# One expert's second, third and fourth tile as a single tile of 320 columns

## The chip, the cores and the metric

The kernel runs on one core of a Trainium2 chip. The core has a matrix engine (TensorE, PE in the profile; its weight loads are listed as PEld), VectorE (DVE), ScalarE (ACT), GpSimd (POOL) and SyncE (SP), which run their own queues of instructions and wait for each other by semaphores. The metric is the device time of one execution in microseconds, the median of several runs.

## The reference

Attention with 32 global and 512 local tokens per batch comes first, then a feed-forward layer with a squared ReLU, then eight routed experts, which are all that the change touches:

```python
def _moe2_ref(x, w_skip, w_gate, w1, w2):          # x: 2176 x 512
    do_compute = x @ w_skip > 0
    out = x.copy()
    xc = x[do_compute]
    logits = xc @ w_gate                            # 8 experts
    e_idx = np.argmax(logits, axis=1)
    probs = softmax(logits)
    gate_w = probs[np.arange(len(xc)), e_idx]
    for e in range(8):
        mask = e_idx == e
        h = np.maximum(xc[mask] @ w1[e], 0.0)       # 512 -> 1024
        y[mask] = gate_w[mask, None] * (h @ w2[e])  # 1024 -> 512
    out[do_compute] = xc + y
```

With the reference's inputs the experts 0 to 7 get 337, 24, 22, 433, 82, 126, 86 and 133 tokens. Expert 3, with 433, is the one that has more than three tiles of 128.

## The kernel before

Each float32 operand of the experts is split into a high part, rounded to the format fp32r that TensorE multiplies fast, and a low part, the rest; a product takes three matmuls (high by high, high by low, low by high). The weights come in eight pieces of 512 KB per expert (`fetch_expert`, on the SP queue), are cast to their high part on ScalarE and subtracted to their low part on VectorE (`convert_expert`; tiles e24h, e24l and so on, eight numbers per expert). `work` spreads this over the steps u of the first tile of an expert, for five pieces of the next expert ahead.

A tile of 128 tokens goes through `gather` (an indirect DMA on GpSimd by the token list), `prepare` (four transposes on TensorE, a copy for the high part on ScalarE, a subtraction for the low part on VectorE) and `expert_tile`: tokens are the stationary operand, weights move with 512 columns (48 matmuls in all), and between the layers the hidden row block is transposed (eight transposes) and split again. The result is multiplied by the gate, added to x (line 950) and scattered to the output (line 954).

How many tiles an expert takes is known only when the kernel runs, so all tiles behind the first stand in nested branches: `more(e, 1)` runs tile 1 if the count is over 128; `more_two(e)` runs tile 2 alone, or, over 384 tokens, tiles 2 and 3 as a pair of 256 columns (`expert_pair`: the weights are stationary in the first layer, the tokens in the second); then tile 4 and a loop. The rows of tile 1 are prepared at step 5 of tile 0, and those of tiles 2 and 3 are gathered and prepared inside tile 1. TensorE's queue is told ahead which way a branch goes by a hint placed by hand (`hint`, at step 0 of the tile before and four steps from the end of the pair).

Everything is emitted in one order written out by hand (`tc.manual_schedule`), so an engine does its work in the order of the lines in the code. The stage around the change is `run(range(AFTER, E), ...)` in the arm `few`, which treats experts 1 and 2 (at most 32 tokens each) in a short form, and then runs the experts 3 to 7 in turn. Tiles of the arm have names ending in `_a`. [...]

Of the kernel before, what the change touches and what calls it, by code (L numbers as in the profile page):

```python
# [54 lines left out]
def attention_ffn_routed_experts(  # L55
# [755 lines left out]
    PARTS_AT = {0: (0, 1), 1: (2,), 2: (3,), 3: (4,), 4: (5,), 5: (6,), 6: (7,)}  # L811
    U0, U1 = 6, 5
    FEW, AFTER = (1, 2), 3
    raws, spare, shared = {}, [], {}

    def give(n):
# [58 lines left out]

    def prepared(e, j):
        if j > 1:
            return [x[:, :, j % 2 * P:(j % 2 + 1) * P] for x in joint()]
        x = xps[(0, e % 2) if j == 0 else (1, 0)]
        return x[:, 0], x[:, 1]  # L880

    def gather(e, j, gi):
        nc.gpsimd.indirect_dma_start(  # L883
# [4 lines left out]
    def prepare(e, j):  # L888
        tr = pair(f"etr_{e}_{j}")
        transposes(tr, gathered(e, j))  # L890
        split(*prepared(e, j), tr)

    def inner(in_arm, z, name):
        tag = ("s", "o")[z % 2] if in_arm else "h"
# [2 lines left out]
    def expert_tile(e, j, si):  # L897

        name = f"{e}_{j}"
        xg, (ph, pl) = gathered(e, j), prepared(e, j)  # L900
        hs, rs = [None] * 2, [None] * 2
        hl = sb("kT", 1, [P, NPAIR, S], f"ehl_{name}").rearrange("p a s -> p (a s)")[:, 0:2 * KE * P].bitcast(F32R)
        gh, gl = (hl[:, z * KE * P:(z + 1) * KE * P].rearrange("p (f k) -> p f k", f=KE) for z in range(2))
        y = ps.tile([P, DM], F32, tag="x2", bufs=2, name=f"y_{name}{arm[0]}")

        def first(fb, k0, k1):
            if k0 == 0:
                hs[fb] = inner(j > (not e), fb, f"eh_{name}_{fb}")
            h = hs[fb]
            for k in range(k0, k1):  # L910
                wh, wl = ew[e, 1, (fb, k)]
                nc.tensor.matmul(h, lhsT=ph[:, k, :], rhs=wh, start=(k == 0), stop=False)
                nc.tensor.matmul(h, lhsT=ph[:, k, :], rhs=wl, start=False, stop=False)
                nc.tensor.matmul(h, lhsT=pl[:, k, :], rhs=wh, start=False, stop=(k == KD - 1))
            if k1 == KD:
                rs[fb] = sb("sm", 2, [P, S], f"er_{name}_{fb}")[:, 0:512]
                nc.scalar.activation(rs[fb], h, AF.Relu)

        def turn(fb):
            tr = pair(f"ertr_{name}_{fb}")  # L920
            transposes(tr, rs[fb])
            split(gh[:, 4 * fb:4 * fb + 4, :], gl[:, 4 * fb:4 * fb + 4, :], tr)

        def second(f0, f1):
            for f in range(f0, f1):
                wh, wl = ew[e, 2, f]
# [145 lines left out]
    with tc.manual_schedule():  # L1072
# [187 lines left out]
        def more(e, j):  # L1260

            if j == UNROLL:
                with tc.For_i(UNROLL, (n_tok[e] + (P - 1)) // P, 1) as it:
                    gi = sb("gi", 2, [P, 1], f"gi{e}", I32)
                    nc.vector.tensor_copy(gi, gidx[:, bass.ds(it + e * TPE, 1)])
                    si = sb("si", 2, [P, 1], f"si{e}", I32)
                    nc.vector.tensor_copy(si, sidx[:, bass.ds(it + e * TPE, 1)])
                    gather(e, UNROLL, gi)
                    prepare(e, UNROLL)
                    for _ in expert_tile(e, UNROLL, si):  # L1270
                        pass
                return
            with tc.If(n_tok[e] > least(e, j), label=f"more{e}_{j}{arm[0]}") as branch:
                if e and j == 4:
                    gather(e, j, slot(gidx, e, j))
                    prepare(e, j)
                    following = ()
                else:
                    following = (2, 3) if e else range(j + 1, UNROLL)[:1]
                for z in following:  # L1280
                    if (e, z) != (0, 3):
# [28 lines left out]
        def run(experts, later=(), ahead=NST - 1, late=U0):  # L1310
            later = list(later)
            for e in experts:
                for u, _ in enumerate(expert_tile(e, 0, slot(sidx, e, 0))):
                    if u in HINTS:
                        hint(e, 1, HINTS[u])
                    if u == U1:
                        prepare(e, 1)
                        if e == E - 1:
                            prepare_rest(e, 1)
                    if u == (U0 if e != experts[0] else late) and e + 1 < E:  # L1320
                        prepare(e + 1, 0)
                    work(e, u, ahead if e == experts[0] else NST - 1)
                    if later:
                        later.pop(0)()
                more(e, 1)

        more(0, 2)
        carried = dict(est), dict(raws)
        shared.update((n, raws[n]) for n in est)
        with tc.If(n_tok[E] <= SEG, label="few") as few:  # L1330
            arm[0] = "_a"
            both_o = sb("xt", 1, [P, 3 * BLK], "eo_few")[0:2 * SEG, 0:DM]
            both_si = sb("hi_i", 2, [P, 1], "si_few", I32)[0:2 * SEG]
            rests = []
# [71 lines left out]
```

## Time and profile before

| | us |
|---|---|
| median of 3 runs | 719.64 (717.83 to 722.03) |
| the profiled execution | 719.74 |
| its span, first to last instruction | 718.0 |
| TensorE busy in the span | 689.4 |
| VectorE busy in the span | 398.7 |
| ScalarE busy in the span | 369.8 |

The profile is of one execution. A time in it counts from the start of the span. A row of the timeline gives the start, the duration, the engine, the line of the code, the operation, the tiles written and read and, in brackets, how long the engine stood idle before and who released it. Matmuls overlap, so their pace is read from their starts. An engine's name with a q stands for its queue: branches, register and semaphore operations.

### The profile page before, as it was taken

How to read it: one execution, taken by the hardware profiler on the slowest of the kernel's cores; microseconds unless marked ns; L12 is line 12 of the kernel's file. 1: busy time of each engine (PE TensorE's matmuls, PEld its weight loads, DVE VectorE, ACT ScalarE, POOL GpSimd, SP SyncE). 2: the span in 40 equal slices, each digit the busy share in tenths (PEclk: the TensorE clock that was granted, in tenths of full speed). 3: DMA queues.
4: the chain of work that ended last, by engine and by line, in shares of the span. 5: the costliest groups of instructions: out<-in, count | busy, mean ns of one | idle time of the engine just before them, and what ended most of it. 6: DMA issues, size and time to landing. Idle time of an engine off the chain costs nothing.

```text
span 718.0 us, 18725 instructions
## 1 busy us (share of the span) xinstructions
PE 689.4 (96%) x7613; PEld 575.8 (80%) x7613; DVE 398.7 (56%) x1067; ACT 369.8 (52%) x943; POOL 165.1 (23%) x209
## 2 busy tenths in 40 slices
PE   7689998999999999999999999999999999999995
PEld 4566677888888988888898898888977887897773
DVE  1889955762654255365336436525267527517993
ACT  5767567665534654444355453534336226416880
POOL 5000053463112221221122212122215224202211
PEclk9799999999999999999999999999999999999999
DMA  9999552064064303115530403110048599905910
GB/s 273 256 294 313 190 132 61 2 167 85 2 145 113 83 32 73 44 36 111 132 65 32 108 2 112 49 59 31 31 147 267 164 324 360 388 26 185 358 34 24
DMA packets 119161, 95.31 MB, mean 133 GB/s; under 512 B 84885, under 2 KB 92053, under 8 KB 119044
## 3 DMA queue, kind: packets, MB, share of 16 engines
q1 hardware_dynamic: 108352, 71.01, 35.3%
q10 hardware_dynamic: 8292, 15.48, 6.5%
q0 software_dynamic: 2400, 7.28, 3.0%
q8 instruction: 71, 1.16, 0.7%
q14 instruction: 46, 0.38, 0.2%
HBM read 81.49 MB, written 12.79 MB: 131 GB/s over the span
## 4 chain that ended last, share of the span: by engine, by line
PE 70%; DMA 17%; issue 5%; DVE 3%; SPq 1%; ACT 1%; POOL 1%; POOLq 0%; ACTq 0%; DVEq 0%
DMA xg<-x2d,slots 15%; PE h L700 8%; PE acc L725 7%; PE acc L727 7%; PE h L702 7%; PE h L701 7%; PE acc L726 7%; PE sc L413 3%; PE acc L723 3%; PE h L697 3%; PE po L451 2%; PE ptr L442 2%; PE gsa L485 1%; PE qtr L341 1%; PE x2tr L280 1%
## 5 line engine op out<-in xcount | busy, mean ns | idle before, releaser
L184 POOL TENSOR_TENSOR gl<-g,gh 128x256 fp32r<-128x256 f32 x107 | 79.5, 743 | 303.1 <-ACT gh L183 146.1
L700 PE MATMUL h<-xh,w_in 128*128 128x256 f32 x464 | 135.0, 291 | 0.7 <-ACT xh L183 0.7
L701 PE MATMUL h<-xl,w_in 128*128 128x256 f32 x464 | 129.7, 280 | 0.3 <-DVE xl L184 0.3
L702 PE MATMUL h<-xh,w_in 128*128 128x256 f32 x464 | 129.8, 280 | 0.0
L725 PE MATMUL acc<-w_out,gh 128*128 128x512 f32 x232 | 97.6, 421 | 1.5 <-ACT gh L183 1.5
L727 PE MATMUL acc<-w_out,gl 128*128 128x512 f32 x232 | 92.0, 396 | 0.2
L726 PE MATMUL acc<-w_out,gh 128*128 128x512 f32 x232 | 91.7, 395 | 0.0
L700 PEld LDWEIGHTS h<-xh,w_in 128*128 128x128 f32 x464 | 87.1, 188 | 4.3 <-ACT xh L183 0.9
L701 PEld LDWEIGHTS h<-xl,w_in 128*128 128x128 f32 x464 | 87.3, 188 | 2.6 <-DVE xl L184 0.5
L704 ACT ACTIVATE g<-h 128x256 f32<-128x256 f32 x128 | 48.7, 381 | 77.0 <-PE h L702 45.7
L702 PEld LDWEIGHTS h<-xh,w_in 128*128 128x128 f32 x464 | 87.1, 188 | 0.0
L433 ACT ACTIVATE sm<-sm,mx 128x128 f32<-128x128 f32 x120 | 46.7, 391 | 49.8 <-DVE mx L431 49.8
L741 DVE TENSOR_TENSOR g<-h,g 128x256 f32<-128x256 f32 x53 | 22.3, 420 | 85.5 <-ACT g L704 85.4
L183 ACT CAST gh<-g 128x256 fp32r<-128x256 f32 x116 | 47.2, 407 | 42.2 <-DVE g L741 40.2
L727 PEld LDWEIGHTS acc<-w_out,gl 128*128 128x128 f32 x232 | 43.5, 188 | 11.9 <-POOL gl L184 1.4
L725 PEld LDWEIGHTS acc<-w_out,gh 128*128 128x128 f32 x232 | 43.6, 188 | 8.6 <-ACT gh L183 1.9
L726 PEld LDWEIGHTS acc<-w_out,gh 128*128 128x128 f32 x232 | 43.8, 189 | 5.7
L426 DVE TENSOR_TENSOR sm<-sc,mask 128x512 f32<-128x512 f32 x30 | 20.6, 688 | 23.9 <-PE sc L413 23.2
L255 POOL TENSOR_TENSOR w_in<-st_raw_in,w_in 128x512 fp32r<-128x512 f32 x10 | 13.0, 1309 | 80.6 <-ACT w_in L251 80.6
L883 POOL DMA_INDIRECT xg<-x2d,slots x16 | 20.0, 1250 | 42.8 <-DVE slots L800 13.1
L413 PEld LDWEIGHTS sc<-kT,qT 64*32 64x32 f32 x2048 | 25.5, 110 | 4.3 <-issue 3.5
L743 ACT ACTIVATE g<-g 128x256 f32<-128x256 f32 x63 | 26.2, 417 | 4.5 <-ACT g L704 2.5
(671 smaller groups left out, 1481.0 us busy)
## 6 DMA issues: line engine op xcount, KB each, us to landing
st_e<-in_moe_w_dram SPq DMA_DIRECT2D x46, 512.0 KB, 7.1
vr<-in_v_l_dram SPq DMA_DIRECT2D x49, 192.0 KB, 4.4
st_raw_in<-in_moe_w_in_dram SPq DMA_DIRECT2D x16, 512.0 KB, 6.7
st_raw_out<-in_moe_w_out_dram SPq DMA_DIRECT2D x16, 512.0 KB, 8.3
st_e<-in_moe_w_dram ACTq DMA_DIRECT2D x12, 512.0 KB, 5.4
x2d<-x ACTq DMA_DIRECT2D x19, 256.5 KB, 3.5
st_gv<-in_v_l_dram SPq DMA_DIRECT2D x8, 512.0 KB, 4.5
out_dram<-x ACTq DMA_DIRECT2D x16, 256.0 KB, 3.5
```

The source lines that it names most:

```text
L183: nc.scalar.copy(hi, src)
L184: (lo_engine or nc.vector).tensor_tensor(out=lo, in0=src, in1=hi.bitcast(F32), op=ALU.subtract)
L413: nc.tensor.matmul(scs[g][SEG * i:SEG * (i + 1), p, cols], lhsT=q[rows, p, SEG * i:SEG * (i + 1)], rhs=kT[b][rows, p, keys], start=True, s ...
L433: nc.scalar.activation(sm[:, hh, :], sm[:, hh, :], AF.Exp, bias=mx[:, hh:hh + 1], scale=SCALE, accum_out=osum[:, 2 * hh + g:2 * hh + g + 1],)
L700: nc.tensor.matmul(h, lhsT=wh, rhs=xh[:, k, :], start=(k == 0), stop=False)
L701: nc.tensor.matmul(h, lhsT=wh, rhs=xl[:, k, :], start=False, stop=False)
L702: nc.tensor.matmul(h, lhsT=wl, rhs=xh[:, k, :], start=False, stop=(k == KD - 1))
L704: nc.scalar.activation(g, h, AF.Relu)
L725: nc.tensor.matmul(acc[z], lhsT=gh[:, c], rhs=wh, start=first_one, stop=False)
L726: nc.tensor.matmul(acc[z], lhsT=gh[:, c], rhs=wl, start=False, stop=False)
L727: nc.tensor.matmul(acc[z], lhsT=gl[:, c], rhs=wh, start=False, stop=last_one)
L743: nc.scalar.activation(square, g, AF.Square)
```

## The change

If expert 3 has 385 to 448 tokens (`wide_count`: seven half tiles), its tiles 1, 2 and 3 are worked as one tile of 320 columns, the third of them with 64 rows.

- The rows of tiles 2 and 3 are gathered at the start of the arm (`gather_wide`), and all three tiles are transposed and split at the steps 5, 6 and 7 of tile 0 (`prepare_wide`: two copies on ScalarE and three subtractions on VectorE for each).
- `wide_tile` has the weights stationary in both layers and 320 token columns moving, so the hidden block needs no transposes between the layers. The second layer's result comes out transposed, in four PSUM tiles of 128 x 320. It is copied to SBUF (two blocks by VectorE, two by ScalarE), turned by twelve transposes, multiplied by the gate and added to x in three steps on VectorE, and scattered in three indirect DMAs.
- The old path, `more(e, 1)`, stands in the `Else` of the branch. The hint at step 0 of tile 0 goes to the new branch.
- `prepared` returns lists of column blocks, and the matmuls of `expert_tile` index them so; the operands are the same.

```diff
+    WIDE = 2 * P + P // 2
...
+    def gather_wide(e):
+
+        gather(e, 2, slot(gidx, e, 2))
+        wide_x[e] = sb("x2", 2, [P, ROW], f"xg_wide{e}")[0:P // 2]
+        nc.gpsimd.indirect_dma_start(
+            out=wide_x[e], out_offset=None, in_=x2d,
+            in_offset=bass.IndirectOffsetOnAxis(ap=slot(gidx, e, 3)[0:P // 2], axis=0),
+            bounds_check=NTOK - 1, oob_is_err=False,
+        )
+
+    def prepare_wide(e, j):
+
+        n = P // 2 if j == 3 else P
+        cols = slice((j - 1) * P, (j - 1) * P + n)
+        tr = pair(f"etr_{e}_{j}w")
+        transposes(tr, wide_x[e] if j == 3 else gathered(e, j), n)
+        high, low = ([x[:, :, cols] for x in xs] for xs in wide_slices())
+        for z in range(2):
+            nc.scalar.copy(high[z], tr[:, 2 * z:2 * z + 2, 0:n])
+        for l, h, k in ((low[0], high[0][:, 0:1], 0), (low[1], high[0][:, 1:2], 1), (low[2], high[1], 2)):
+            w = l.shape[1]
+            nc.vector.tensor_tensor(out=l, in0=tr[:, k:k + w, 0:n], in1=h.bitcast(F32), op=ALU.subtract)
+
+    def wide_tile(e):
+
+        xh, xl = wide_inputs(0, WIDE)
+        gs, yt = {}, []
+
+        def first(f):
+            fb, c = divmod(f * P, DM)
+            h = inner(True, f, f"ewh_{e}_{f}")[:, 0:WIDE]
+            for k in range(KD):
+                wh, wl = (w[:, c:c + P] for w in ew[e, 1, (fb, k)])
+                nc.tensor.matmul(h, lhsT=wh, rhs=xh[k], start=(k == 0), stop=False)
+                nc.tensor.matmul(h, lhsT=wh, rhs=xl[k], start=False, stop=False)
+                nc.tensor.matmul(h, lhsT=wl, rhs=xh[k], start=False, stop=(k == KD - 1))
...
+            nc.scalar.activation(gh, h, AF.Relu)
+            nc.vector.scalar_tensor_tensor(
+                out=gl, in0=h, scalar=0.0, in1=gh.bitcast(F32), op0=ALU.max, op1=ALU.subtract
+            )
+
+        def second(f):
...
+            for d in range(KD):
+                wh, wl = (w[:, d * P:(d + 1) * P] for w in ew[e, 2, f])
+                nc.tensor.matmul(yt[d], lhsT=wh, rhs=gh, start=(f == 0), stop=False)
+                nc.tensor.matmul(yt[d], lhsT=wl, rhs=gh, start=False, stop=False)
+                nc.tensor.matmul(yt[d], lhsT=wh, rhs=gl, start=False, stop=(f == KE - 1))
+
+        first(0)
+        for f in range(KE):
+            if f + 1 < KE:
+                first(f + 1)
+            second(f)
...
+        trs = [pair(f"ewtr_{e}_{t}") for t in range(2)]
+        trs.append(inner(True, 0, f"ewtr_{e}_2").rearrange("p (d c) -> p d c", d=KD))
+        for d in range(KD):
+            if d < 2:
+                nc.vector.tensor_copy(ys[:, d], yt[d])
+            else:
+                nc.scalar.copy(ys[:, d], yt[d])
+            for t in range(3):
+                n = P // 2 if t == 2 else P
+                nc.tensor.transpose(trs[t][0:n, d, :], ys[:, d, t * P:t * P + n], ident)
...
+        for t, o in enumerate(os):
+            xg = wide_x[e] if t == 2 else gathered(e, t + 1)
+            n = xg.shape[0]
+            nc.vector.scalar_tensor_tensor(
+                out=o, in0=trs[t].rearrange("p d c -> p (d c)")[0:n], scalar=xg[:, DM:DM + 1], in1=xg[:, 0:DM],
+                op0=ALU.mult, op1=ALU.add,
+            )
+        for t, o in enumerate(os):
+            scatter_rest(o, slot(sidx, e, t + 1)[0:o.shape[0]])
...
                     if u in HINTS:
-                        hint(e, 1, HINTS[u])
-                    if u == U1:
+                        if is_wide(e):
+                            tc.mark_branch_hint_location(f"wide{e}", hint=wide_count(e), engines=HINTS[u])
+                        else:
+                            hint(e, 1, HINTS[u])
+                    if is_wide(e):
+                        if U1 <= u < U1 + 3:
+                            prepare_wide(e, u - U1 + 1)
+                    elif u == U1:
                         prepare(e, 1)
...
-                more(e, 1)
+                if is_wide(e):
+                    with tc.If(wide_count(e), label=f"wide{e}") as wide:
+                        wide_tile(e)
+                    with wide.Else():
+                        more(e, 1)
+                else:
+                    more(e, 1)
+
+        def wide_count(e):
+            return (n_tok[e] + (P // 2 - 1)) // (P // 2) == 7
...
             arm[0] = "_a"
+            gather_wide(AFTER)
```


## Rows read from the trace of the kernel before

**Rows 1.** Page, first part: busy time, share and instructions of each engine.

```profile
PE 689.4 (96%) x7613; PEld 575.8 (80%) x7613; DVE 398.7 (56%) x1067; ACT 369.8 (52%) x943; POOL 165.1 (23%) x209
```

**Rows 2.** By stretch: length, busy PE PEld DVE ACT POOL, PEclk, DMA share, GB/s.

```profile
614.81:627.74 12.93, 12.93 (x68) 10.66 (x66) 4.59 (x7) 4.13 (x7) 3.05 (x3) 1.00 1.04 389
627.74:651.02 23.28, 22.83 (x145) 20.09 (x143) 5.38 (x12) 3.39 (x9) 1.11 (x2) 1.00 0.08 29
651.02:664.34 13.32, 13.17 (x64) 10.54 (x65) 11.34 (x13) 10.77 (x14) 4.71 (x4) 1.00 0.79 254
```

**Rows 3.** Timeline of PE in the pair: matmuls of 256, then of 512 columns.

```profile
628.14 0.28 PE L972 MATMUL eph_a<-xp,e24l_a 128*128 128x256 f32 x1
...
630.73 0.40 PE L986 MATMUL yp_a<-e28h_a,egh_a 128*128 128x512 f32 x1
...
632.13 0.28 PE L970 MATMUL eph_a<-xp,e24h_a 128*128 128x256 f32 x1
```

**Rows 4.** Timeline of PE at the two edges of the stage.

```profile
614.46 0.60 PE L280 MATMUL etr_a<-ident,xg 128*128 128x128 f32 x4
614.81 0.48 PE L912 MATMUL eh_a<-e24h_a,xp 128*128 128x512 f32 x1
...
650.18 0.40 PE L988 MATMUL yp_a<-e31h_a,egl_a 128*128 128x512 f32 x1
651.02 0.50 PE L912 MATMUL eh_a<-e32h_a,xp 128*128 128x512 f32 x1 [0.45 <-PEq L1273]
```

**Rows 5.** Groups by line and shape, in 614.81 to 651.02.

```profile
L975 DVE SCALAR_TENSOR_TENSOR egl_a<-eph_a,egh_a 128x256 fp32r<-128x256 f32 x8 | 3.4, 425 | 16.6 <-ACT egh_a L974 16.6
L974 ACT ACTIVATE egh_a<-eph_a 128x256 fp32r<-128x256 f32 x8 | 3.1, 384 | 18.0 <-PE eph_a L972 18.0
...
L184 DVE TENSOR_TENSOR xp<-etr_a,xp 128x512 fp32r<-128x512 f32 x3 | 2.1, 689 | 2.3 <-ACT xp L183 2.3
...
L183 ACT CAST xp<-etr_a 128x512 fp32r<-128x512 f32 x3 | 1.8, 587 | 3.2 <-PE etr_a L280 3.2
```

**Rows 6.** Timeline of VectorE in tile 0 and at the seam, and e34l's reader.

```profile
611.29 1.21 DVE L845 TENSOR_TENSOR e31l_a<-st_e,e31h_a 128x1024 fp32r<-128x1024 f32 x1
...
614.26 1.22 DVE L845 TENSOR_TENSOR e33l_a<-st_e,e33h_a 128x1024 fp32r<-128x1024 f32 x1
...
649.91 1.45 DVE L999 SCALAR_TENSOR_TENSOR eop_a<-yp_a,xg 128x512 f32<-128x512 f32 x2 [1.26 <-PE yp_a L988]
651.79 1.22 DVE L845 TENSOR_TENSOR e34l_a<-st_e,e34h_a 128x1024 fp32r<-128x1024 f32 x1 [0.43 <-DVEq L1273]
...
654.16 0.40 PE L913 MATMUL eh_a<-e34l_a,xp 128*128 128x512 f32 x1
```

**Rows 7.** Timeline of POOL: gathers in the arm's start and behind tile 0.

```profile
602.71 2.42 POOL L883 DMA_INDIRECT xg<-x2d,slots  x1 [8.43 <-PE y_rest_a L1054]
...
617.76 1.02 POOL L883 DMA_INDIRECT xg<-x2d,slots  x1 [0.31 <-DMA xg<-x2d,slots]
```

**Rows 8.** Branches and hints of PE's queue by line, ns min/median/max, when.

```profile
L1273 PEldq COMPARE_BRANCH  x1: 200/200/200, 650.8 to 650.8; - x1
...
L1273 PEldq COMPARE_BRANCH  x1: 335/335/335, 661.7 to 661.7; - x1
...
L1292 PEldq COMPARE_BRANCH  x1: 4920/4920/4920, 709.9 to 709.9; - x1
...
L1401 PEldq BRANCH_PREFETCH_HINT  x8: 35/38/44, 579.7 to 691.8; - x8
```

**Rows 9.** Page, third part: a queue that fetches instructions, packets, MB.

```profile
q8 instruction: 71, 1.16, 0.7%
```

**Rows 10.** Busy time and granted clock (PEclk) by stretch, as in rows 2.

```profile
26.30:33.10 6.80, 5.47 (x80) 3.91 (x84) 5.89 (x14) 6.02 (x22) 0.00 (x0) 0.50 1.10 272
...
710.60:715.70 5.10, 0.00 (x0) 0.00 (x0) 1.38 (x4) 0.00 (x0) 0.89 (x1) 1.00 0.07 15
715.80:718.00 2.20, 0.00 (x0) 0.00 (x0) 0.00 (x0) 0.00 (x0) 0.00 (x0) 0.50 0.01 4
```

More of the change, by code (lines that the diff above doesn't have):

```diff
@@ L877, in prepared, with is_wide @@
         if j > 1:
-            return [x[:, :, j % 2 * P:(j % 2 + 1) * P] for x in joint()]
-        x = xps[(0, e % 2) if j == 0 else (1, 0)]
-        return x[:, 0], x[:, 1]
+            x = [x[:, :, j % 2 * P:(j % 2 + 1) * P] for x in joint()]
+        else:
+            if j == 1 and is_wide(e):
+                return wide_inputs(0, P)
+            x = xps[(0, e % 2) if j == 0 else (1, 0)]
+            x = x[:, 0], x[:, 1]
+        return [[z[:, k] for k in range(KD)] for z in x]
+    def is_wide(e):
+        return e == AFTER and arm[0] == "_a"
@@ new lines, in wide_slices, with wide_inputs @@
+    def wide_slices():
+        a, b, c = (
+            xps[i].rearrange("p a k c -> p (a k c)")[:, 0:3 * WIDE].rearrange("p (k c) -> p k c", k=3)
+            for i in ((1, 0), (2, 0), (2, 1))
+        )
+        return (a[:, 0:2], b[:, 0:2]), (a[:, 2:3], b[:, 2:3], c[:, 0:2])
+    def wide_inputs(c0, c1):
+        high, low = wide_slices()
+        return [[x[:, k, c0:c1] for x in xs for k in range(x.shape[1])] for xs in (high, low)]
+    wide_x = {}
+    def gather_wide(e):
[6 more added lines that the diff above has]
+        )
@@ new lines, in wide_tile @@
+    def wide_tile(e):
[9 more added lines that the diff above has]
+                nc.tensor.matmul(h, lhsT=wl, rhs=xh[k], start=False, stop=(k == KD - 1))
+            gh = sb("pT", 2, [P, 4, P], f"ewgh_{e}_{f}").rearrange("p a k -> p (a k)")[:, 0:WIDE].bitcast(F32R)
+            gl = sb("sm", 2, [P, S], f"ewgl_{e}_{f}")[:, 0:WIDE].bitcast(F32R)
+            gs[f] = gh, gl
+            nc.scalar.activation(gh, h, AF.Relu)
[3 more added lines that the diff above has]
+        def second(f):
+            gh, gl = gs.pop(f)
+            if f == 0:
+                for d in range(KD):
+                    tag = ("x2", "h")[d // 2]
+                    yt.append(ps.tile([P, DM], F32, tag=tag, bufs=2, name=f"ewy_{e}_{d}{arm[0]}")[:, 0:WIDE])
+            for d in range(KD):
[8 more added lines that the diff above has]
+            second(f)
+        ys = sb("kT", 1, [P, NPAIR, S], f"ewys_{e}").rearrange("p a s -> p (a s)")[:, 0:KD * WIDE]
+        ys = ys.rearrange("p (d c) -> p d c", d=KD)
+        trs = [pair(f"ewtr_{e}_{t}") for t in range(2)]
+        trs.append(inner(True, 0, f"ewtr_{e}_2").rearrange("p (d c) -> p d c", d=KD))
+        for d in range(KD):
+            if d < 2:
[5 more added lines that the diff above has]
+                nc.tensor.transpose(trs[t][0:n, d, :], ys[:, d, t * P:t * P + n], ident)
+        os = [sb("xt", 1, [P, 3 * BLK], f"ewo_{e}_0")[:, 0:DM], sb("x2", 2, [P, ROW], f"ewo_{e}_1")[:, 0:DM]]
+        os.append(wide_x[e][:, 0:DM])
+        for t, o in enumerate(os):
[4 more added lines that the diff above has]
+                op0=ALU.mult, op1=ALU.add,
+            )
+        for t, o in enumerate(os):
+            scatter_rest(o, slot(sidx, e, t + 1)[0:o.shape[0]])
@@ L890, in prepare @@
         transposes(tr, gathered(e, j))
-        split(*prepared(e, j), tr)
+        if j > 1:
+            split(*(x[:, :, j % 2 * P:(j % 2 + 1) * P] for x in joint()), tr)
+        else:
+            x = xps[(0, e % 2) if j == 0 else (1, 0)]
+            split(x[:, 0], x[:, 1], tr)
     def inner(in_arm, z, name):
@@ L911, in first @@
                 wh, wl = ew[e, 1, (fb, k)]
-                nc.tensor.matmul(h, lhsT=ph[:, k, :], rhs=wh, start=(k == 0), stop=False)
-                nc.tensor.matmul(h, lhsT=ph[:, k, :], rhs=wl, start=False, stop=False)
-                nc.tensor.matmul(h, lhsT=pl[:, k, :], rhs=wh, start=False, stop=(k == KD - 1))
+                nc.tensor.matmul(h, lhsT=ph[k], rhs=wh, start=(k == 0), stop=False)
+                nc.tensor.matmul(h, lhsT=ph[k], rhs=wl, start=False, stop=False)
+                nc.tensor.matmul(h, lhsT=pl[k], rhs=wh, start=False, stop=(k == KD - 1))
             if k1 == KD:
@@ L1280, in more @@
                 for z in following:
-                    if (e, z) != (0, 3):
+                    if (e, z) not in ((0, 3), (e if is_wide(e) else E, 2)):
                         gather(e, z, slot(gidx, e, z))
@@ L1314, in run @@
                     if u in HINTS:
-                        hint(e, 1, HINTS[u])
-                    if u == U1:
+                        if is_wide(e):
+                            tc.mark_branch_hint_location(f"wide{e}", hint=wide_count(e), engines=HINTS[u])
+                        else:
+                            hint(e, 1, HINTS[u])
[3 more added lines that the diff above has]
+                    elif u == U1:
                         prepare(e, 1)
@@ L1324, in run @@
                         later.pop(0)()
-                more(e, 1)
+                if is_wide(e):
[3 more added lines that the diff above has]
+                        more(e, 1)
+                else:
+                    more(e, 1)
+        def wide_count(e):
+            return (n_tok[e] + (P // 2 - 1)) // (P // 2) == 7
         more(0, 2)
```

## The prediction

> **What bounds the kernel now.** I read the page first: TensorE is busy 96% of the span [rows 1]. A share over the whole span does not say what the change's stage is worth, so I cut the stage of expert 3 into its stretches [rows 2]. In tile 1 TensorE is busy in all of 12.93 us, in the pair of tiles 2 and 3 in 22.83 of 23.28, at the full clock. VectorE and ScalarE work a third of that time or less. So TensorE's own columns set this stage, and every microsecond taken from them moves all that follows, as long as nothing else comes last.
>
> Next I took TensorE's timeline for the price of a matmul. Starts, not durations, are what counts, since matmuls overlap: 22 matmuls of 256 columns start in 630.73 - 628.14 = 2.59 us, 117.7 ns each; six of 512 columns in 632.13 - 630.73 = 1.40 us, 233.3 ns each [rows 3]. Both lie on one line, 0.4516 ns a column and 2 ns besides. At the stage's edges [rows 4], expert 3's tile 1 starts at 614.81, right behind four transposes that take 0.35 us. The last matmul of the pair starts at 650.18, and expert 4's first at 651.02: 0.84 us, of which 0.23 is the matmul's own place, so leaving the stage costs 0.61 us.
>
> **The change, part by part.** The stage takes 651.02 - 614.81 = 36.21 us now.
>
> *Columns.* Before: 48 matmuls of 512 (11.20 us), 96 of 256 (11.30) and 48 of 512 (11.20). After: 96 + 96 of 320. No row has 320 columns; the bounds are the rows at 117.7 and 233.3 ns, and since these lie on a line I take 146.6 ns, 192 x 0.1466 = 28.15 us. That is 5.55 us less. At the bounds the stage would be 5.5 us shorter still or 16.6 us longer.
>
> *Transposes moved and added.* Eight transposes of r in tile 1 go. Those of tiles 2 and 3 move into tile 0, the last of them and expert 4's now standing between tile 0's last matmul and the new tile: 0.36 us for tile 2 (with 0.09 us a transpose as in rows 4), about 0.3 for the 64 rows of tile 3. The new tile could start at 615.5, not 614.81. Twelve transposes come at the end: 12 x 0.09 = 1.07 us. Their copies hide: output block 3 is copied last, on ScalarE, some 0.45 us by [rows 5] (384 ns at 256 columns, 587 at 512), while nine transposes fill 0.8 us. Without that cover it would cost 0.3 us.
>
> *Splits.* Each tile's rows are split by three subtractions on VectorE. From 425 ns at 256 columns and 689 at 512 [rows 5] I estimate 0.76 us per tile where 0.61 stood, and 0.14 + 0.14 + 0.21 for the 64 rows. VectorE's queue in tile 0 has no air: e31l runs from 611.29 for 1.21 us, and e33l starts at 614.26, with the split of tile 1 (0.61) and e32l (1.13) between them [rows 6]. In the new order come tile 1's split, e32l, tile 2's split, e33l, tile 3's split: 612.45 + 0.76 + 1.13 + 0.76 + 1.13 = 616.23, and with the first low part 616.5. TensorE's first matmul needs only high parts (ScalarE has them by about 615.5), the second needs that low part and would be due at 615.65. So it waits 0.85 us. Bounds: 0, if VectorE runs ahead of this, and 1.7, if one more subtraction of 1.13 us gets in front. What is queued behind on VectorE, tile 0's output and expert 4's split, has no reader before the next expert.
>
> *Gathers moved.* Two gathers go from behind tile 0's scatter (the first at 617.76) to the start of the arm. POOL stands idle there for 8.43 us ahead of the gather at 602.71 [rows 7]; at 1.0 to 2.4 us each they fit. Were that cover gone, expert 4's rows would land some 5 us later, still ahead of their transposes at 614.46. I cost it at nothing. SP's queue is not passed.
>
> *The way out.* This is what I find most doubtful. The wide tile stands in an If whose Else holds the whole old path; TensorE, having run the wide tile, must jump over that path: 48 + 144 + 2 x 48 matmuls of three tiles and the pair, another 48 in the loop, their weight loads and transposes, some 790 instructions. The trace has jumps of three kinds [rows 8]. One at 650.8, over a few instructions and without a hint, took 0.200 us; it is in the 0.61 above. One announced by a hint took 0.335 us at 661.7, over the same path of expert 4. The one at the end of the kernel, over the untaken arm and unannounced, took 4.92 us. All eight hints of the trace are those written out by hand, and the change marks the If's entry alone. So the new jump is unannounced like the last row and some three instruction blocks long (71 blocks in 1.16 MB [rows 9], 16 KB each). Bounds 0.2 and 4.92; it is nearer to the second, but shorter, and fewer engines fetch at once, so I take 3.9: 3.7 us more than the jump it replaces. [...]
>
> [...]
>
> *VectorE at the seam.* Three outputs of 0.75 us instead of two (1.45) come behind the transposes: about 645.6 to 647.7, then 0.43 us for the branch as now (651.36 to 651.79), and e34l done at 649.4. TensorE reads it 654.16 - 651.02 = 3.14 us after it starts expert 4 [rows 6]. With a slow jump that hides; with a quick one it costs 0.1.
>
> **The sum.** 615.5 + 0.15 + 0.85 + 191 x 0.1466 = 644.5; transposes to 645.57; leaving as now, 646.2; jump, 649.9. Expert 4 starts 1.1 us earlier than at 651.02, and experts 4 to 7 shift with it: their weights are ahead, since the queues moved only 29 GB/s during the pair [rows 2]. The profiled execution took 719.74 us, 1.7 of it outside the span, and the median of the runs is 719.64: the same. 719.74 - 1.1 = 718.6. The three runs before lie 0.6% apart, so 0.5%, 3.6 us, is about what can be told from no change.
>
> **Rivals.**
> 1. *The exit jump is cheap* (0.2 to 0.34 us). Then expert 4 starts at 646.2, 4.8 us earlier: 714.9, or 714.0 if the splits come in time as well. For it: the 0.200 us row and the hinted one. Against it: nothing announces the jump, and the end of the kernel shows what that can cost. If only VectorE's own jump stalls, e34l comes some 3 us late and this case falls back to about 717.8.
> 2. *The exit takes the full 4.92 us and the clock falls: slower.* Expert 4 then starts at 650.9, so the whole gain is spent. TensorE would have stood still from 645.6 on. At the end of the trace the granted clock was still 1.00 in the 5.1 us after the last matmul and 0.50 behind them; early on, among short matmuls, it was 0.50 for 6.8 us [rows 10]. [...] Half the clock for 6.8 us costs 3.4: 723.0 us, and 723.9 with the longer wait for splits. It decides only with a hole as long as that one of 5.1 us; against it, I expect one of about 4. [...]
> 3. *A matmul of 320 columns takes more than its place on the line.* From 152 ns on the gain of 1.1 us is gone; at 180 ns, half way up to the 512-column row, the time is 725.0 us. Against it: both measured widths lie on one line.
>
> **Chances.** My forecast (a slow exit, between 717 and 720): 0.60. Rival 1: 0.29. Rival 2: 0.07, half of it beyond 0.5%. Rival 3: 0.04. Faster by over 0.5% (below 716.0) is rival 1 but for its VectorE variant, 0.26, and 0.04 from a forecast whose jump is at its shortest: 0.30. Slower by over 0.5% (above 723.3): 0.035 + 0.035 = 0.07. Within: 0.63. The range leaves out the lower edge of rival 1 and most of rivals 2 and 3: 714.3 to 721.3. The forecast's own range is 717.0 to 720.2.
>
> **What would show it.** In the profile after: 192 matmuls of 320 columns, starts 147 ns apart; one wait of some 0.85 us at the second of them, put down to VectorE; 12 transposes without a gap; and behind them a hole on TensorE, with a branch of 3 to 5 us in its sequencer. If the hole is under 1 us, the prediction is wrong by some 4 us; if the wide matmuls start more than 152 ns apart, or the clock dips behind the hole, it is wrong the other way.

## The result, and the profile after

The changed kernel takes 724.34 us (median of 6 runs, 723.62 to 725.42), the kernel before 719.93 us beside it (717.83 to 722.03): a ratio of 1.0063, 95% interval 1.0042 to 1.0085. It is slower by 0.6%, where 718.6 us and a range of 714.3 to 721.3 were predicted. The profiled execution took 724.18 us with a span of 722.5.

First the stretches, as in [rows 2]: expert 3's tile 0, the wide tile with its exit, then experts 4, 5, 6, 7 and the rest.

```profile
602.25:616.25 14.00, 14.00 (x76) 11.28 (x73) 13.04 (x21) 9.65 (x16) 7.73 (x4) 1.00 1.05 378
616.25:649.43 33.18, 29.89 (x206) 29.39 (x204) 10.25 (x21) 6.95 (x14) 2.03 (x2) 1.00 0.41 153
649.43:664.31 14.88, 14.73 (x64) 11.67 (x65) 9.77 (x12) 9.09 (x12) 4.93 (x3) 0.89 0.72 212
664.31:681.25 16.94, 14.99 (x64) 11.65 (x65) 12.67 (x14) 11.19 (x15) 4.64 (x5) 0.90 0.94 315
681.25:695.99 14.74, 13.32 (x64) 10.43 (x65) 13.85 (x15) 11.16 (x16) 2.56 (x2) 1.00 0.33 115
695.99:709.15 13.16, 13.16 (x65) 10.43 (x65) 9.30 (x10) 7.82 (x11) 1.02 (x1) 1.00 0.06 18
709.15:722.50 13.35, 4.32 (x99) 2.82 (x98) 2.55 (x6) 0.38 (x1) 1.88 (x2) 0.82 0.08 27
```

From the start of tile 0 to expert 4 it is 14.00 + 33.18 = 47.18 us, 1.9 less than before (601.91 to 651.02, 49.11). Up to there the change pays, and a little more than predicted. Everything is lost behind it: from expert 4 to the end it is 73.1 us where it was 67.0, 6.1 more. Expert 4's tile takes 14.88 (13.32 before), expert 5's 16.94 (13.46), expert 6's 14.74 (13.90). In the first two the granted clock is below 1.00 (0.89 and 0.90), and in expert 5's and 6's TensorE stands idle for longer (1.95 and 1.42 us; 0.15 and 0.60 before).

TensorE's timeline at the entry and the exit of the wide tile, and its branch:

```profile
616.25 0.38 PE L937 MATMUL ewh_a<-xp,e24h_a 128*128 128x320 f32 x1
616.92 0.41 PE L938 MATMUL ewh_a<-xp,e24h_a 128*128 128x320 f32 x1 [0.29 <-DVE xp L925]
617.17 0.31 PE L939 MATMUL ewh_a<-xp,e24l_a 128*128 128x320 f32 x1
617.32 0.31 PE L937 MATMUL ewh_a<-xp,e24h_a 128*128 128x320 f32 x1
...
644.96 1.47 PE L976 MATMUL ewtr_a<-ident,ewys_a 128*128 128x128 f32 x12
649.43 0.73 PE L1023 MATMUL eh_a<-e32h_a,xp 128*128 128x512 f32 x1 [3.00 <-issue]
```

```profile
L1443 PEldq COMPARE_BRANCH  x1: 3742/3742/3742, 645.6 to 645.6; - x1
```

From the third wide matmul, at 617.17, to the transposes at 644.96 it is 190 matmuls, 146.3 ns each. The branch that ends the wide tile takes 3.742 us in TensorE's queue, and TensorE's array stands still for 3.00 us of it. Right behind this hole the granted clock is 0.50 for 3.40 us, and once more in expert 5:

```profile
649.50:652.90 3.40, 3.40 (x8) 2.68 (x9) 2.21 (x2) 0.00 (x0) 1.77 (x1) 0.50 0.60 179
670.00:673.40 3.40, 3.40 (x12) 2.72 (x11) 2.06 (x3) 1.09 (x2) 0.00 (x0) 0.50 0.97 338
```

Expert 5 needs a second look, since its stall begins on another engine. GpSimd's timeline first, then VectorE's, then TensorE's:

```profile
647.28 1.00 POOL L1132 DMA_INDIRECT out_dram<-ewo_a,slots  x1 [28.11 <-DVE ewo_a L982]
650.80 1.77 POOL L1132 DMA_INDIRECT out_dram<-ewo_a,slots  x1 [2.52 <-DVE e35l_a L846]
660.85 1.51 POOL L1132 DMA_INDIRECT out_dram<-xg_wide_a,slots  x1 [8.28 <-DVE ehl_a L184]
662.67 1.66 POOL L990 DMA_INDIRECT xg<-x2d,slots  x1 [0.30 <-issue]
```

```profile
667.04 0.75 DVE L1061 SCALAR_TENSOR_TENSOR eo_a<-y_a,xg 128x512 f32<-128x512 f32 x1 [1.79 <-DMA out_dram<-xg_wide_a,slots]
668.10 1.23 DVE L846 TENSOR_TENSOR e42l_a<-st_e,e42h_a 128x1024 fp32r<-128x1024 f32 x1 [0.31 <-ACT er_a L1028]
```

```profile
667.19 0.40 PE L1023 MATMUL eh_a<-e42h_a,xp 128*128 128x512 f32 x1
669.38 0.50 PE L1024 MATMUL eh_a<-e42l_a,xp 128*128 128x512 f32 x1 [1.80 <-DVE e42l_a L846]
```

The reader is to follow it backwards. TensorE waits for e42l, the low half of a weight piece. VectorE makes it late because, ahead of it in its queue, the output of expert 4 waits for the third scatter of the wide tile to land. The third scatter goes out at 660.85 only, ten microseconds behind the second: GpSimd's queue stands in a wait for 9.465 us from 650.7 on, until about 660.2, and the second scatter, issued at 650.80, takes 9.3 us to land, at about 660.1. All three write the output tensor. In these 9.3 us, while expert weights are being loaded, the DMA share is 0.68 (before, the second scatter took 6.4 us, beside a share of 0.96; why it takes longer now is not shown). Behind the third on GpSimd's queue stands the gather of expert 6's rows, at 662.67. In the kernel before, with two scatters, it went out at 656.84:

```profile
650.94 1.00 POOL L1003 DMA_INDIRECT out_dram<-eop_a,slots  x1 [20.94 <-DVE eop_a L999]
654.55 1.59 POOL L1003 DMA_INDIRECT out_dram<-eop_a,slots  x1 [2.61 <-DVE e35l_a L845]
656.84 1.05 POOL L883 DMA_INDIRECT xg<-x2d,slots  x1 [0.69 <-issue]
```

Last, a branch at the end of expert 6's tile. It is announced by a hint like those of experts 4, 5 and 7, which take 0.36 to 0.46 us, and yet takes 3.75 (0.354 before), by the maximum in this row; TensorE loses 1.42 us of it:

```profile
L1384 PEldq COMPARE_BRANCH  x4: 362/420/3751, 661.6 to 706.6; - x4
```

```profile
695.99 0.47 PE L1023 MATMUL eh_a<-e56h_a,xp 128*128 128x512 f32 x1 [1.42 <-PEq L1384]
```

### The profile page after: what moved, and what is told of

It is laid out like the page before. It is cut to its first block, busy times and chain, and to the rows that moved or that the text cites. A ratio compares the mean times of both kernels' runs of the same rounds, so it can differ in the third digit from the quotient of the medians.

```text
span 722.5 us, 18733 instructions
## 1 busy us (share of the span) xinstructions
PE 687.0 (95%) x7617; PEld 576.4 (80%) x7617; DVE 398.3 (55%) x1073; ACT 368.7 (51%) x944; POOL 167.3 (23%) x209
```

## The experiments

Two theories came out of this. A: the hole at the exit, with the half clock behind it, spent the gain. B: the chain of scatters on GpSimd did, through VectorE's wait. The rival to both is that the other one alone is enough, or that the loss only moves to the next place. Later a theory C was added for expert 6's branch: where the code lies.

This table has for every kernel the median, the ratio to the kernel before on the same chip, and from its profiled execution the time from TensorE's first matmul of expert 3 to that of expert 4, of the tiles of experts 4 to 7, and from there to the end of the span (differences of the starts in TensorE's timeline, us). Stalls are in bold. The ratio is worked out from the runs of both kernels and is not the quotient of the two medians; the kernel before took 719.3 to 720.6 us on these chips, so rows from different chips are compared by their ratios.

| kernel | median | ratio (95%) | 3 | 4 | 5 | 6 | 7 | rest |
|---|---|---|---|---|---|---|---|---|
| before | 719.93 | 1 | 49.11 | 13.32 | 13.46 | 13.90 | 13.33 | 12.94 |
| changed | 724.34 | 1.0063 (1.0042 to 1.0085) | **47.18** | **14.88** | **16.94** | **14.74** | 13.16 | 13.31 |
| e1_exit | 722.44 | 1.0030 (1.0014 to 1.0045) | 43.93 | 13.60 | **19.42** | **14.50** | 13.15 | 13.82 |
| e2_own_buffer | 721.28 | 1.0008 (0.9989 to 1.0027) | **47.09** | **14.86** | 13.47 | **15.00** | 13.20 | 14.12 |
| e3_exit_own | 717.88 | 0.9969 (0.9950 to 0.9989) | 43.93 | 13.61 | **14.37** | **14.15** | 13.14 | 13.47 |
| e4_two_scatters | 720.42 | 0.9987 (0.9966 to 1.0008) | **47.01** | 13.33 | 13.46 | **14.68** | 13.15 | 14.31 |
| e5_busy | 721.16 | 1.0009 (0.9994 to 1.0023) | **49.10** | 13.32 | 13.49 | 13.46 | 13.35 | 13.39 |
| e6_late_hint | 719.36 | 0.9985 (0.9968 to 1.0003) | 43.93 | 13.60 | **20.39** | **14.28** | 13.14 | 13.52 |
| e7_early_split | 719.41 | 0.9998 (0.9982 to 1.0014) | 43.33 | 13.60 | **16.59** | **14.38** | 13.15 | 13.30 |
| e8_scatter_later | 717.45 | 0.9964 (0.9950 to 0.9978) | 43.94 | 13.60 | 13.63 | **14.60** | 13.33 | 14.13 |
| e8_again | 717.89 | 0.9949 (0.9929 to 0.9969) | 43.95 | 13.60 | 13.53 | **14.69** | 13.14 | 13.92 |
| e9_code_shift | 718.91 | 0.9999 (0.9973 to 1.0026) | **45.65** | 13.60 | 13.93 | 13.48 | 13.33 | 13.93 |
| e10_later_shift | 718.05 | 0.9977 (0.9961 to 0.9992) | 43.94 | 13.60 | **15.65** | 13.29 | 13.39 | 13.58 |
| e3_again | 718.41 | 0.9984 (0.9961 to 1.0006) | 43.95 | 13.59 | **14.05** | **14.83** | 13.15 | 13.94 |
| e11_all_four | 717.55 | 0.9969 (0.9954 to 0.9984) | **45.75** | 13.60 | 13.45 | 13.47 | 13.33 | 12.95 |
| e12_shift_behind | 717.69 | 0.9962 (0.9941 to 0.9984) | 43.94 | 13.61 | 13.46 | 13.48 | **14.50** | 13.44 |

The last column differs by up to 1.4 us. Up to 0.5 us of it is a wait of TensorE for ScalarE in the last short tile, the remainder lies behind the last matmul; neither was followed.

**e1_exit: the jump alone.** The arms are swapped, so that the wide tile lies last and runs on into expert 4 without jumping over the old path. The condition is turned round with them (`not_wide`), in the hint too.

```diff
-                    with tc.If(wide_count(e), label=f"wide{e}") as wide:
-                        wide_tile(e)
-                    with wide.Else():
-                        more(e, 1)
+                    with tc.If(not_wide(e), label=f"wide{e}") as narrow:
+                        more(e, 1)
+                    with narrow.Else():
+                        wide_tile(e)
```

> The two arms of the branch change places: the old path is the first arm, the wide tile the Else, entered by a hinted jump, and its exit is short. Theory A (the hole at the exit and the half clock behind it are the loss): TensorE's hole of 3.0 us goes, expert 4 starts some 3 us earlier at the full clock, 724.3 - 3.2 - 1.7 = about 719.4 us. Theory B (the chain of the three scatters on POOL decides what follows): the hole goes as well, but VectorE can still not write expert 4's output before the third scatter has landed at about 666.7, so its next weights are no earlier and TensorE waits about 5 us there in place of 1.8: 722 to 724.5 us.

The hole at the exit is gone: the transposes run straight into expert 4, whose tile takes 13.60 us at the full clock. The jump has moved to the entry of the wide tile, which a hint announces, and takes 0.448 us there. But expert 5 loses more than before:

```profile
664.11 0.40 PE L1023 MATMUL eh_a<-e42h_a,xp 128*128 128x512 f32 x1
668.78 0.50 PE L1024 MATMUL eh_a<-e42l_a,xp 128*128 128x512 f32 x1 [4.28 <-DVE e42l_a L846]
```

Counted from expert 3's start, TensorE comes to e42l 4.5 us earlier and waits 4.28 us in place of 1.80, so more than half of what the exit gave is taken back. Only 1.9 us of the median are won: the time lies where theory B put it, not A.

**e2_own_buffer: VectorE's wait alone.** The output tile of expert 4 shared its buffer with the first output tile of the wide tile; it gets another.

```diff
-        o = sb("xt", 1, [P, 3 * BLK], f"eo_{name}")[:, 0:DM]
+        if (e, j) == (AFTER + 1, 0):
+            o = sb("pT", 2, [P, 4, P], f"eo_{name}").rearrange("p a k -> p (a k)")
+        else:
+            o = sb("xt", 1, [P, 3 * BLK], f"eo_{name}")[:, 0:DM]
```

> Expert 4's output goes to another buffer (the tag pT, free since the wide tile) and so has nothing to do with the scatters. Theory A (exit hole): no change, 724 us. Theory B (scatter chain): VectorE's wait of 1.8 us in expert 4 goes, TensorE's wait for e42l goes, and so does the second stretch at half clock: 724.3 - 1.8 - 1.7 = about 720.8 us.

VectorE's output of expert 4 waits for nothing now, and expert 5 takes 13.47 us. The hole at the exit stays, with the half clock behind it:

```profile
649.23 0.50 PE L1023 MATMUL eh_a<-e32h_a,xp 128*128 128x512 f32 x1 [2.91 <-issue]
```

```profile
650.70:654.10 3.40, 3.40 (x9) 2.63 (x8) 0.90 (x1) 0.50 (x2) 1.77 (x1) 0.50 0.81 267
```

**e3_exit_own: both.**

> Both: the arms changed over, and expert 4's output in another buffer. If the two losses are independent links of one chain, this gains more than the sum of the two alone: expert 4 starts at about 646.3, both stretches at half clock go, 724.3 - 3.2 - 1.7 - 1.8 - 1.7 = about 715.9 us, 0.5% under the kernel before. If theory A alone holds it is 719.4, if theory B alone 720.8.

717.88 us: faster than before, but 2 us above what was expected. It is 6.5 us below the changed kernel, where the two edits alone won 1.9 and 3.1. By the ratios that is 0.94%, and 0.79% in e3_again, where the two alone won 0.33 and 0.55%: so the times do not show that both together win more than the sum. The profiles, one of each, do: from the start of expert 3 to the end of the span, e1_exit is 1.8 us shorter than the changed kernel, e2_own_buffer 2.5, and both together 7.5, or 6.7 in e3_again. The two are links of one chain: without the own buffer, more than half of what TensorE gains at the exit it waits for at e42l. In the profile the clock is 1.00 through expert 7; 0.69 us are left in expert 5, where the transposes wait for the late gather of expert 6's rows, and expert 6's branch stays long (3.167 us). Run again on another chip (e3_again) it gave 718.41 us and a ratio whose interval reaches 1; its longest times were 721 to 724 us.

> The kernel with both mends once more, unchanged, beside the three others: 717.9 us again, 0.2 to 0.5% below the kernel before; above 719 us if its gain was due to the chip it ran on.

**e4_two_scatters: the third scatter left out.** Here 49 rows of expert 3 are not written; all else is the changed kernel.

```diff
-        for t, o in enumerate(os):
+        for t, o in enumerate(os[:2]):
```

> The third scatter of the wide tile is left out, so 49 rows of the output are not written; all else as in the changed kernel. Theory B (scatter chain): VectorE's wait in expert 4 goes with it, about 720.8 us. If VectorE waits there for other transfers (the weights that are loaded at the same time), the wait stays and the time is 724 us.

Expert 5's stall is gone, as with the own buffer, so it takes both the shared buffer and the third scatter. The gathers of the next rows go out from 653.38 us on, not 662.67: nothing but that scatter held them.

```profile
653.38 1.05 POOL L990 DMA_INDIRECT xg<-x2d,slots  x1 [0.30 <-issue]
```

Why VectorE, which needs the buffer of the first output tile, waits until the third scatter has landed, the runs don't show. The hole at the exit is there, but in this execution the clock did not fall behind it, and expert 4's tile takes 13.33 us:

```profile
649.76 0.50 PE L1023 MATMUL eh_a<-e32h_a,xp 128*128 128x512 f32 x1 [2.83 <-issue]
```

**e5_busy: work for the array during the jump.** e2_own_buffer, with 15 float32 matmuls behind the twelve transposes.

```diff
+        for _ in range(15):
+            nc.tensor.matmul(busy, lhsT=ident, rhs=ident, start=True, stop=True)
```

> The kernel with the output of expert 4 in a buffer of its own, and 15 float32 matmuls of 128x128 (a product that nobody reads) queued on TensorE behind the twelve transposes, in the arm of the wide tile, so that TensorE's array has work queued when its sequencer comes to the exit jump. If the idle of about 3 us behind the jump is what lets the granted clock fall to 0.5, no stretch of 0.5 follows, the tile of expert 4 takes about 13.3 us and not 14.9, and the time is about 721.3 - 1.6 = 719.7 us. If the clock falls for another reason, or if the sequencer only comes to the jump when the array is nearly done with that work, so that it hides nothing, the stretch stays and the time is 721.3 to 722 us.

```profile
652.48 0.50 PE L1026 MATMUL eh_a<-e32h_a,xp 128*128 128x512 f32 x1 [1.56 <-ACT e36h_a L840]
```

The branch still takes 3.657 us, but the array is idle for 1.56 us only, the clock does not fall, and expert 4's tile takes 13.32 us, as expected of the first theory. That the shorter idle time is the reason is not shown, since the clock held in e4_two_scatters too. The time did not fall to the 719.7 us expected (721.16 us): the added work of 3.5 us delays the jump, and expert 3 takes 2.0 us longer than in e2_own_buffer. (The 15 matmuls stand in the trace as 30 records with a weight load each; they run for 3.51 us in all, 0.23 us for one float32 matmul of 128 columns, where one of 320 columns of the split operands takes 0.146.) Expert 6's branch became short here (0.447 us) although nothing was changed there but the place of its code and the moment at which it is reached, which led to theory C.

**e6_late_hint and e7_early_split.** On e3_exit_own: the hints of experts 4 to 7 at step 2 of a tile, not step 0; and, on top, the wide tile's transposes and splits at steps 4 to 6 of tile 0 (this second edit is shown).

```diff
-                        if U1 <= u < U1 + 3:
-                            prepare_wide(e, u - U1 + 1)
+                        if U1 - 1 <= u < U1 + 2:
+                            prepare_wide(e, u - U1 + 2)
```

> The kernel with both mends (arms swapped, output of expert 4 in a buffer of its own), and the hints of the branches of expert 4 and later given at step 2 of an expert's first tile in place of step 0. Theory one: the branch at the end of expert 6's tile takes 3.2 to 4.0 us because its hint comes while TensorE's sequencer is fetching instructions in order, and is lost; then the branch takes 0.3 to 0.5 us here, the gap of 1.2 us on TensorE at the start of expert 7 goes, and the time is about 717.9 - 1.2 = 716.7 us. Theory two: it is where the code lies, or the distance from hint to branch, that matters; then the branch stays at 3 to 4 us (or another one takes its place) and the time is 717.5 to 718.3 us.

> As the kernel with both mends and the late hints, with the transposes of the wide tile's rows and their splits put at steps 4 to 6 of the tile ahead of it in place of 5 to 7. If the splits are late for the wide tile's first matmuls, the wait of about 0.3 us at its second matmul goes and the distance from the tile ahead to the wide tile falls from 14.0 to about 13.5 us: 0.3 to 0.7 us below the kernel with late hints alone. If the gather of the rows lands too late for the earlier place, TensorE waits for it there, and the time is the same or up to 1 us above.

The late hint changed nothing: expert 6's branch takes 3.486 us. That theory fell. What shows in e6_late_hint's profile is the late gather: GpSimd issues it at 662.81, behind the third scatter, and TensorE stands for 4 us, with the clock at half for 6.8 us from 672.7:

```profile
673.89 1.09 PE L280 MATMUL etr_a<-ident,xg 128*128 128x128 f32 x4 [4.08 <-DMA xg<-x2d,slots]
```

With the early splits the wait at the second wide matmul is gone and expert 3 takes 0.60 us less (43.33 for 43.93), as expected; but the branch of expert 5 takes 5.616 us there and TensorE loses 3.00 us at it, so the whole time says nothing about the splits. The same branch took 0.445 us in e6_late_hint, although e7 only changes the order of TensorE's work inside expert 3's tile 0 and adds none to it. The branches of experts 4 to 7 in e6 and e7, shortest, median and longest:

```profile
L1387 PEldq COMPARE_BRANCH  x4: 375/440/3486, 657.5 to 705.4; - x4
```

```profile
L1387 PEldq COMPARE_BRANCH  x4: 362/2000/5616, 657.7 to 701.9; - x4
```

**e8_scatter_later: the queue on GpSimd.** On e3_exit_own, the third scatter is issued at step 3 of expert 4's tile, behind its two gathers.

```diff
-        for t, o in enumerate(os):
+        for t, o in enumerate(os[:2]):
             scatter_rest(o, slot(sidx, e, t + 1)[0:o.shape[0]])
+        late_scatter.append(lambda: scatter_rest(os[2], slot(sidx, e, 3)[0:P // 2]))
...
+                    if u == 3 and late_scatter and e == AFTER + 1 and arm[0] == "_a":
+                        late_scatter.pop()()
```

> The kernel with both mends (arms swapped, output of expert 4 in a buffer of its own), and the third scatter of the wide tile issued behind expert 4's two gathers in place of ahead of them. If the wait of that scatter for the second one holds up the gather of expert 6's rows behind it on GpSimd's queue (issued at 659.42 us with both mends, at 656.84 us before), the gather goes out about 5 us earlier, expert 6's transposes no longer wait for it (0.7 us with both mends; 4.1 us in the profile of the late hints), expert 6 starts 13.4 to 13.6 us after expert 5, and the time is 0.7 to 1.5 us below that of both mends beside it. If the gather lands late because of the weight loads it shares the DMA engines with, an earlier issue changes little: the wait stays within 0.5 us and the time is the same.

```profile
655.26 1.94 POOL L991 DMA_INDIRECT xg<-x2d,slots  x1 [0.30 <-PE eh_a L1026]
657.50 1.02 POOL L991 DMA_INDIRECT xg<-x2d,slots  x1 [0.30 <-issue]
664.04 0.94 POOL L1136 DMA_INDIRECT out_dram<-xg_wide_a,slots  x1 [5.52 <-issue]
```

The gathers are out before the third scatter, and no transpose of expert 5's tile waits for them. The median is 0.4 to 1.0 us below e3_exit_own's two; run again it gave 717.89 us, and the intervals of the ratios overlap, so the medians alone do not tell the two kernels apart. The longest times differ more: 719.05 to 720.35 us in the five rows with the third scatter behind the gathers (e8, e8_again, e10, e11, e12), 720.84 to 725.48 in the five with both mends and the scatter ahead of them (e3, e3_again, e6, e7, e9). Of these five only the longest of e6, 723.28, is a profiled one: it is the execution in which TensorE stands 4.08 us for the late gather. The chain can still bite one place further on. In e8's own profile expert 4's scatter goes out at 670.75 only, behind the third; VectorE's output of expert 5 waits 1.02 us for it to land, and TensorE 1.04 us for e50l. This is expert 6's stall in that row; in e8_again it is the branch.

> The kernel with three mends again, unchanged, beside the one before: 717.4 us again, 0.2 to 0.5% below the kernel before.

**e9_code_shift, e10_later_shift, e11_all_four, e12_shift_behind: the place of the code.** Matmuls in an arm that does not run move all later instructions of TensorE. e9 has 16 on top of e3_exit_own, e10 has 40 on top of e8_scatter_later, e11 16 on top of that kernel, all three in expert 3's arm; e12 has 16 in expert 4's arm, behind the wide tile.

```diff
                     with tc.If(not_wide(e), label=f"wide{e}") as narrow:
+                        unused = inner(True, 0, f"unused_{e}")
+                        for _ in range(16):
+                            nc.tensor.matmul(unused[:, 0:P], lhsT=ident, rhs=ident, start=True, stop=True)
                         more(e, 1)
```

> The kernel with both mends, and 16 float32 matmuls in the arm that does not run (experts' tiles of 128 and 256 rows for expert 3), so that all instructions of TensorE behind it, those of experts 4 to 7 among them, lie some 64 instructions further on; nothing that runs is changed. If the long branch at the end of expert 6's tile (3.2 us with both mends, hinted as the others, which take 0.4 us) comes from where its code lies, it becomes 0.3 to 0.5 us here or another hinted branch becomes long in its place; without a long one the time is 1.2 us below both mends beside it. If it comes from the order of hints and branches in time, it stays at 3 to 4 us at the same place.

> Both mends, the third scatter behind expert 4's gathers, and 40 float32 matmuls in the arm that does not run (a shift of some 160 instructions). By the theories of the two kernels before this one that hold, their gains add: if both do, 716 us or below and no gap of over 1 us on TensorE between the wide tile and the rest; if only the scatter's does, as that kernel alone within 0.5 us.

> All four mends in one kernel: arms swapped, output of expert 4 in a buffer of its own, the third scatter behind expert 4's gathers, and the 16 float32 matmuls in the arm that does not run. If each of the four takes a stall of its own, none is left between the wide tile and the rest: experts 4 to 7 take 13.3 to 13.7 us each, no gap of over 1 us stands on TensorE there, and the time is 1.2 us below that with three mends (717.45 us), about 716.3 us, 0.4 to 0.6% below the kernel before. If the stalls trade places, one of 1 us or more shows up elsewhere, and the time is 717 to 718 us.

> As the kernel with three mends (arms swapped, own buffer, third scatter behind the gathers), and the 16 float32 matmuls that never run put into the arm of expert 4 that does not run, in place of expert 3's: the wide tile and expert 4's tile lie where they lie with three mends, experts 5 to 7 lie 64 instructions further on. If both stalls come from where the code lies, neither the stall in the wide tile (1.5 us with all four) nor the long branch at the end of expert 6 (2.2 to 3.8 us with two or three mends) is there, and the time is 1.0 to 1.5 us below that of three mends beside it. If the stall only changes its place again, it shows up at another branch and the time is the same within 0.5 us.

Each shift moves the long branch or does away with it. The four hinted branches of experts 4 to 7, shortest, median and longest, in e9, e10 and e12, one row of each kernel:

```profile
L1387 PEldq COMPARE_BRANCH  x4: 348/404/475, 658.0 to 698.9; - x4
```

```profile
L1388 PEldq COMPARE_BRANCH  x4: 356/410/4657, 657.7 to 700.1; - x4
```

```profile
L1388 PEldq COMPARE_BRANCH  x4: 356/420/3355, 657.8 to 698.2; - x4
```

In e9 none is long, and in e11 none either (0.475 us at most in both); in e10 it is expert 5's, in e12 expert 7's. In the ten profiles of kernels to which no code was added, the changed kernel's among them, it is expert 6's (in e7 expert 5's as well). So moving the code moves the stall (theory C). But the place of a branch's own code does not decide alone. In e11 and e12 the code of experts 5 to 7 lies equally far on, and expert 7's branch takes 0.368 us in one and 3.355 in the other; e7 makes expert 5's long without moving it. What else counts, the runs leave open. And e9 and e11 have a hole inside the wide tile instead, at its first matmul of the second layer, which the kernels without that shift do not have:

```profile
622.53 0.42 PE L956 MATMUL ewy_a<-ewgh_a,e28h_a 128*128 128x320 f32 x1 [1.54 <-issue]
```

That is e11; nothing that the profile shows is waited for (in e9 ScalarE is named, but it had been done for 0.9 us). The stall trades places, and no shift that was tried is without one. In time none of them won: e9 was expected 1.2 us below e3_again and is 0.5 above, e10 is 0.6 above e8, and e11 and e12 lie between e8's two medians. The best kernels, e8, e11 and e12, agree within 0.45 us, with ratios to the kernel before of 0.9949 to 0.9969.

## Why the prediction was wrong

**Right, or nearly.** *Columns*: 146.3 ns where 146.6 was taken; rival 3 is out. *The way out*: 3.742 us where 3.9 was taken, the hole 3.00 us long. The 3.9 was the author's estimate between two rows, lowered for a jump of some three blocks and for fewer engines fetching at once; that either of these makes a jump shorter, no run shows. From 645.6 to 649.4, while the branch stands, q8, the queue in [rows 9], moved one packet of 0.02 MB; what the time goes to is not shown. Rival 1, the cheap exit, did not happen, and e1_exit shows what it would have been worth: expert 3 and its exit take 43.93 us, 3.25 less, but only 1.9 us reach the median.

**Off in size.** *Transposes*: from tile 0 to the wide tile it took 14.00 us where 12.90 + 0.70 was expected; the last four transposes alone are followed after 0.51 us (615.74 to 616.25), not 0.35. *Splits*: the wait at the second wide matmul is 0.29 us, not 0.85; from the first wide matmul to the twelve transposes it took 28.71 us, not 29.0. *The way out* makes the larger difference: from these transposes to expert 4 it took 4.47 us, not 5.4. The sum let nothing cover the jump, which no run shows: the branch begins at 645.6 and the array works until 646.4, so 0.7 of its 3.742 us are covered, and in e5_busy, with more work queued, 2.1 of 3.657. Together expert 4 starts 47.18 us behind tile 0 of expert 3, not 48.0: 0.8 us better than the sum.

**The step that failed** is in *The sum*: "experts 4 to 7 shift with it". Its reason, "their weights are ahead", looked at SP's queue alone. Three things behind expert 4's start cost 5.9 of the 6.1 us:

- The three scatters. *Gathers moved* counted GpSimd's gathers; the scatters that the new tile issues at its end stand in no term. Before, there were two at this place, and the wait for the second to land is not seen to hold anything up (the gathers follow at 656.84). The third waits for the second, holds the gathers behind it, and through a shared buffer VectorE's output of expert 4. This is expert 5's 3.5 us, the second fall of the clock included; e2_own_buffer and e4_two_scatters each take it away.
- The clock behind the hole, 1.6 us in expert 4's tile. It was priced in rival 2, but only for a hole of about 5 us, with a chance of 0.07. It came at 3.00 us, and at 2.91 in e2_own_buffer; e5_busy, which shortens the idle time to 1.56, is without it, but so is e4_two_scatters with 2.83. What makes it fall stays open.
- The branch of expert 6, 0.8 us against before. It moves when code is moved; why it is the one that gets long stays open.

The time of rival 2 (723.0 to 723.9) came close to 724.34, but not by its mechanism: the exit took less than it asked for, and more than half of the loss is the scatters'.

**Open.** Expert 3 starts between 601.2 and 604.6 us in these kernels and at 601.91 in the one profile of before; this spread of up to 3.4 us lies ahead of the change and was not traced. It may be why the profiles from expert 3 on show 3.5 and 3.6 us won by e11 and e12, and the medians 1.8 and 2.9.

## What to carry to other kernels

A new path in a branch is costed with all that it queues on every engine at its end: here one more scatter in a chain, on an engine that is 23% busy, cost 3.5 us, more than the 1.9 that the change had won by the start of expert 4. Put the path that will run last in the branch, so that it leaves by running on and only the hinted entry jumps (0.448 us in e1_exit, for the exit's 3.742). And when one stall is removed, look for the next wait of the same chain before judging the edit: with the exit mended alone, TensorE's wait for e42l grew from 1.80 to 4.28 us, and with both mends 0.69 us of waiting were left in that tile.

## What was not expected of the hardware

- The clock fell to half behind idle times of TensorE of 3.00, 1.80 (changed kernel), 2.91 (e2) and 4.28 us (e1), and within one of 4.08 (e6), and not behind 2.83 (e4), 3.00 (e7), 2.33 (e10) and 1.56 us (e5). In these rows the length of the idle time alone does not decide.
- The branches of experts 4 to 7, which a hint announces, took 0.335 to 0.478 us in the kernel before (0.362 to 0.457 and one of 3.751 in the changed one); the long ones took 2.247 (e8) to 5.616 us (e7), and moving code changed which one was long. In the variants that were run one such branch, or two (e7), was long, but for e9 and e11 with the hole in the wide tile and e5 with its long exit.
- At this place an indirect scatter went out only when the one before it, to the same tensor, had landed. Before, the first landed 2.8 us after its issue and the second went out after 3.6; in the changed kernel the second landed after 9.3 us and the third went out after 10.05, beside weight loads. The gathers behind a scatter did not wait for it to land: before, the second scatter, issued at 654.55, landed after 6.4 us, and the gathers went out at 656.84 and 658.19. That the shared tensor is the reason was not tested.
